# A tuned mixer and gated MLP block on one core: down products added to the output by adding DMAs, in 2x2 block form for all tokens, with the work of the MLP loop spread one slot apart

## The chip, the core and the metric

The kernel runs on one core of a Trainium2 chip. The metric is the device time of one execution in microseconds (us). Before the change the median of three runs is 1683.22 us (1682.0 to 1684.33). All matrix products are of 128 rows by 128 columns of weights against 512 tokens, in float32 rounded to a short form ("high") plus a remainder ("low").

## The reference, cut to what matters

```python
g = sigmoid((x * gate_w).sum(-1, keepdims=True))
a = linear_attention(x, wqkv, w_phi) @ wo          # 32 heads, per-head softmax feature maps
gate = x @ W_gate ; up = x @ W_up                  # x: 2048 x 576, W_gate, W_up: 576 x 4608
h = relu(gate) * up
out = g * a + (1 - g) * (h @ W_down)               # W_down: 4608 x 576
```

The kernel folds 1 - g into x ahead of the MLP (its square root into each factor), and keeps the output transposed: 576 rows, 2048 tokens.

## The kernel before

**Two stages.** The first makes the attention part and, in `project_out`, writes g * a transposed to a DRAM tile `att`. The second is the MLP, a loop `chunk(u)` over 72 units. A unit is one half of the tokens (`hf`, 1024 tokens, two blocks `t` of 512) and one of 36 chunks of 128 hidden columns; u = 0 to 35 work on the first half, 36 to 71 on the second. Two units make a group `g`, 36 groups in all.

**A unit's products.** Gate and up of a chunk for both token blocks are a 2x2 by 2x2 block product, done with seven products of sums and differences of blocks (in place of eight). `SEQ = (1, 5, 6, 2, 7, 3, 4)` is their order, one in each of a unit's seven slots, each of seven matmuls (`product`). The products accumulate in three PSUM tiles: `cx` (1, 6, 7, 4), `ca` (5, 3) and `cy` (2). ScalarE (ACT) copies `cx` or `ca` out while it still grows (tiles `g1`, `u2`, `g2`), VectorE (DVE) adds the rest, applies the gate, and `high_h`/`low_h` split a hidden tile into `hh` (ACT) and `hl` (DVE).

**Weights of the products.** For u below 36, the raw chunk `wr` is loaded, and unit u prepares the operands of unit u + 1: `blocks` (three blocks, high on ACT, low on DVE), `sums_of_blocks` (four DVE operations in place), `block_sums` (four sums, high and low). These operands, tiles `wb` and `ws`, are also written to DRAM (`wbd`, `wsd`), and the second half of the tokens loads them from there (`load_operands`).

**Down products.** Behind each slot's product stands a down product of the group before. For groups of the first half, `down_plain` multiplies plain blocks: eight slots of a group with six matmuls, and two with four for the last 64 output rows (`pm`): 56 matmuls. For groups of the second half, `down` uses the seven-product form for each half `m` of the output rows: 14 slots with three matmuls, four of them with two more for the last rows: 50 matmuls. Its weights need sums of blocks (`down_sums_of_blocks`, on GpSimd, POOL) and sums of hidden tiles. Both accumulate in two PSUM banks, `chain` and `other`, and DVE adds each bank into an accumulator `ac` in SBUF one slot later (L920 and L952). The accumulators are loaded from `att`, and stored to the output at the end of a token half.

**Order.** `in_order` keeps every engine's instructions in the order in which the Python code issues them, so an instruction that waits holds up all that stand behind it on its engine. Some of a unit's work is handed over to the next unit in lists (`CARRY`). In units 4 to 16 POOL also scales and subtracts x for the second half of the tokens (`second_half`, tiles `xb`, L296 and L301).

Of the kernel before, what the change touches and what calls it, by code (L numbers as in the profile page):

```python
# [7 lines left out]
F32 = mybir.dt.float32  # L8
# [54 lines left out]
def gated_mix_kernel(  # L63
# [33 lines left out]
    att = dram.tile([D, S], F32, name="att")  # L97
# [4 lines left out]
    wbd = dram.tile([NC, P, 3, 5, P], F32, name="wbd")  # L102
    wsd = dram.tile([NC, P, 4, 5, P], F32, name="wsd")
# [486 lines left out]
    def project_out(tb):  # L590
        oh, ol = OW.pop(tb)
        ts = slice(tb * TB, (tb + 1) * TB)
        for m in range(5):
# [17 lines left out]
            nc.sync.dma_start(att[m * P:m * P + n, ts], o)  # L611
# [96 lines left out]

    def load_operands(u):

        c = units[u][1]
        b, o = wop.tile([P, 3, 5, P], F32R, name="wb"), wop.tile([P, 4, 5, P], F32R, name="ws")
        nc.sync.dma_start(b.bitcast(F32), wbd[c])
        nc.sync.dma_start(o.bitcast(F32), wsd[c])
        WO[u] = {1: (b, 0), 2: (b, 1), 4: (b, 2), 5: (o, 2), 6: (o, 0), 7: (o, 3), 3: (o, 1)}
# [72 lines left out]
    tp = ctx.enter_context(tc.tile_pool(name="tp", bufs=7, **CB))  # L788
    ac = ctx.enter_context(tc.tile_pool(name="ac", bufs=1, **CB))
# [9 lines left out]
    LAST = {3: (0, 1), 2: (0, 0), 7: (1, 1), 4: (1, 0)}  # L799
    WDR, WD, W4, HID, ACC, ACC4, BANK, REST = {}, {}, {}, {}, {}, {}, {}, {}  # L800
# [3 lines left out]
    def load_down(g):  # L804
        if g < 2 * NG:
            WDR[g] = wdp.tile([P, 9 * P], F32, name="wdr", bufs=1)
            nc.sync.dma_start(WDR[g], wd[g % NG])
# [7 lines left out]
    def down_blocks(g, m, f):  # L815

        if f is high:
            o = down_tile()
# [37 lines left out]
    def plain_down(g, f):  # L856

        if f is high:
            o = down_tile()
            WD[g] = o[:, :16 * P].rearrange("p (s q) -> p s q", s=2)  # L860
            W4[g] = o[:, 16 * P:].rearrange("p (b s q) -> p b s q", b=2, s=2)
        f(WD[g], WDR[g][:, :8 * P])
        f(W4[g].rearrange("p b s q -> p s b q"), WDR[g][:, 8 * P:].rearrange("p (b q) -> p b q", b=2))

# [15 lines left out]
    def load_acc(hf, i, m, t):  # L880
        a = ACC[hf, i, m, t] = ac.tile([P, TB], F32, name=f"ac{i}{m}{t}")
        nc.sync.dma_start(a, att[rows(i, m, t, hf)])

    def load_rest(hf):
        for t in range(2):
            a = ACC4[hf, t] = ac.tile([64, TB], F32, name=f"ar{t}")
            nc.sync.dma_start(a, att[4 * P:, rows(0, 0, t, hf)[1]])

    PLAIN = {1: (0, 0, 1), 2: (0, 1, 1), 3: (2, 0, 1), 4: (0, 0, 0), 5: (0, 1, 0), 6: (2, 0, 0),
             8: (1, 0, 1), 9: (1, 1, 1), 11: (1, 0, 0), 12: (1, 1, 0)}  # L890

    def down_plain(g, s):

        if s not in PLAIN:
            return lambda: []
        i, m, t = PLAIN[s]
        first, last = g == 0, g == NG - 1
        mms = []
        if i == 2:
            if first:  # L900
                REST[t] = pm.tile([P, TB], F32, name=f"pm{t}")
            ps = REST[t]
            for c in range(2):
                w = W4[g][:, c].rearrange("p s q -> p (s q)")
                mms += [(w, v) for v in HID[g, c, t]]
        else:
            ps = pd.tile([P, TB], F32, name="chain" if s % 2 else "other")
            for c in range(2):
                b = 4 * m + (c if i == 0 else 3 - c)
                w = slice(b * P, (b + 1) * P)  # L910
                h, l = HID[g, c, t]
                mms += [(WD[g][:, 0, w], h), (WD[g][:, 0, w], l), (WD[g][:, 1, w], h)]
        for k, (w, v) in enumerate(mms):
            nc.tensor.matmul(ps, w, v, start=k == 0 and (i < 2 or first),  # L914
                             stop=k == len(mms) - 1 and (i < 2 or last), skip_group_check=True)

        def add():
            if i < 2:
                a = ACC[0, i, m, t]
                tt(out=a, in0=ps, in1=a, op=ADD)  # L920
                if last:
                    return [(0, i, m, t)]
            return []
        return add

    def down(g, s, bank):
# [22 lines left out]
        def add():  # L949
            i, t = ADDS[n]  # L950
            a = ACC[hf, i, m, t]
            tt(out=a, in0=ps, in1=a, op=ADD)  # L952
            return [(hf, i, m, t)] if last and LAST.get(n) == (i, t) else []
        return add

    def store(keys):
        for hf, i, m, t in keys:
            nc.sync.dma_start(out[rows(i, m, t, hf)], ACC.pop((hf, i, m, t)))
            if hf == 0:
                load_acc(1, i, m, t)  # L960

    def rest_rows(hf, t):

        b = tp.tile([64, TB], F32, name="b", tag="tp")
        nc.scalar.activation(b, REST[t][64:], AF.Copy)
        tt(out=b, in0=REST[t][:64], in1=b, op=ADD)
        for a in (ACC4[hf, 0], ACC4[hf, 1])[t:t + 1 if hf == 0 else 2]:
            pt(out=a, in0=a, in1=b, op=ADD)

    def store_rest(hf, t):  # L970
        nc.sync.dma_start(out[4 * P:, rows(0, 0, t, hf)[1]], ACC4[hf, t])

    def one_bank(m, n):
        key = "chain" if n == 1 else "other"
# [41 lines left out]
    CARRY = {j: [] for j in range(7)}  # L1016
    PEND = []

    def chunk(u):
        hf, c = units[u]  # L1020
        g, odd = divmod(u, 2)
        v = u + 1
        make = 0 < u < NC - 1
        plain = hf == 0
        done = []

        def slot(j, ps, n, first):

            product(ps, u, n, first)
            if PEND:  # L1030
                done.extend(PEND.pop()())
            if g > 0:
                q = g - 1
                PEND.append(down_plain(q, 7 * odd + j) if q < NG else down(q, 7 * odd + j, one_bank))
            store(done)
            done.clear()
            if u == 1 and j == 0:
                CARRY[3] += CARRY[0]
                CARRY[0].clear()
            work = CARRY[j][:]  # L1040
            CARRY[j].clear()
            for f in work:
                f()


        cx = px.tile([P, TB], F32, name="cx")
        slot(0, cx, 1, True)
        if u == 1:
            nc.sync.dma_start(wbd[u], WB.pop(u).bitcast(F32))
        if make:  # L1050
            blocks(v, high_w)
        elif NC - 1 <= u < 2 * NC - 1:
            load_operands(v)
        g1 = tp.tile([P, TB], F32, name="g1", tag="tp")
        nc.scalar.activation(g1, cx, AF.Copy)
        if make:
            blocks(v, low_w)
            blocks(v, low_w_rows)
        swap_in(u, 0)
        if u == 0:  # L1060
            next(early, None)

        ca = pa.tile([P, TB], F32, name="ca")
        slot(1, ca, 5, True)
        if u == 1:
            nc.sync.dma_start(wsd[u], WS.pop(u).bitcast(F32))
        if make:
            sums_of_blocks(v)
        u2 = tp.tile([P, TB], F32, name="u2", tag="tp")
        nc.scalar.activation(u2, ca, AF.Copy)  # L1070
        swap_in(u, 1)
        if u == 0:
            next(early, None)

        slot(2, cx, 6, False)
        if make:
            nc.sync.dma_start(wbd[v], WB.pop(v).bitcast(F32))
            block_sums(v, high_w)
        g2 = tp.tile([P, TB], F32, name="g2", tag="tp")
        nc.scalar.activation(g2, cx, AF.Copy)  # L1080
        if odd and plain and g > 0:
            plain_down(g, high)
        elif odd and g > 0:
            down_blocks(g, 0, high)
            down_blocks(g, 0, low)
            rest_weights(g, 0)
            rest_weights(g, 1)
        if units[u] == (1, 1):
            rest_rows(0, 0)
        swap_in(u, 2)  # L1090
        if u == 0:
            next(early, None)

        cy = py.tile([P, TB], F32, name="cy")
        slot(3, cy, 2, True)
        if odd and plain and g > 0:
            plain_down(g, low)
        elif odd and g > 0:
            down_sums_of_blocks(g, 0)
        tt(out=g1, in0=cy, in1=g1, op=ADD)  # L1100
        swap_in(u, 3)
# [233 lines left out]
```

## Time and profile before

| | |
|---|---|
| median of the runs | 1683.22 us |
| the profiled execution, and its span | 1685.55 us, 1683.8 us |
| mean granted TensorE clock in it | 0.983 |
| first matmul of the MLP loop | 417.06 us |
| last matmul | 1678.34 us |
| DVE, ACT, POOL busy over the span | 1256.9, 592.3, 213.8 us |

The loop has some three quarters of the span. A view by windows gives, for a stretch of time, each engine's busy time and the number of its instructions that began there. Matmuls are pipelined: a row of one matmul says 0.39 us, but the next begins 0.227 us after it, so the number of matmuls in a window tells more than the busy time.

### The profile page before, as it was taken

What the parts mean: (1) busy time and instruction counts of PE and PEld (TensorE: products, weight loads), DVE (VectorE), ACT (ScalarE), POOL (GpSimd) and SP (SyncE); (2) the same over time, 40 slices, a digit from 0 to 9 for tenths busy, and PEclk for the clock granted to TensorE, in tenths of its full rate; (3) what the DMA queues carried; (4) which work ended last, traced back from release to release, by engine and by line L of the source; (5) the groups of instructions that cost most, each with busy time, mean ns of one, the idle gap of its engine ahead of it and who ended that gap; (6) DMA issues with size and microseconds to landing.
All of it is one profiled execution on the core that took longest, in us unless ns stands there. A gap on an engine that the chain in (4) does not pass through costs nothing.

```text
span 1683.8 us, 20063 instructions
## 1 busy us (share of the span) xinstructions
PE 1624.7 (96%) x7726; PEld 1357.8 (81%) x7726; DVE 1256.9 (75%) x1881; ACT 592.3 (35%) x962; POOL 213.8 (13%) x257
## 2 busy tenths in 40 slices
PE   8999998798999999999999999999999999999997
PEld 8898996666787878777888887788888888888886
DVE  4878766565777887887877777677777777777777
ACT  4234336554333333233332333332333233323322
POOL 0118210002002010111000000311111111111111
PEclk9899998799999999999999999999999999999999
DMA  7214213544965556656655557654444434343432
GB/s 259 63 44 159 68 38 102 166 148 144 359 223 198 205 194 217 245 192 211 220 187 205 183 199 273 217 210 157 159 151 151 163 153 154 148 167 148 160 142 71
DMA packets 64476, 288.42 MB, mean 171 GB/s; under 512 B 6826, under 2 KB 16426, under 8 KB 55164
## 3 DMA queue, kind: packets, MB, share of 16 engines
q1 hardware_dynamic: 64380, 287.14, 47.6%
q8 instruction: 60, 0.98, 0.2%
q14 instruction: 36, 0.29, 0.1%
HBM read 174.30 MB, written 110.85 MB: 169 GB/s over the span
## 4 chain that ended last, share of the span: by engine, by line
PE 65%; DVE 6%; DMA 2%; ACT 2%; issue 1%; SPq 0%; ACTq 0%; DVEq 0%
PE cx L874 24%; PE ca L874 12%; PE cy L874 6%; PE chain L937 5%; PE other L914 5%; PE chain L914 5%; PE other L937 4%; PE pm L937 2%; PE pm L914 1%; DVE wb L680 1%; DVE wb L683 1%; DMA xt<-xb 1%; ACT wb L677 1%; DVE ac L952 1%; DVE wr L698 0%
## 5 line engine op out<-in xcount | busy, mean ns | idle before, releaser
L981 ACT ACTIVATE hh<-g 128x512 fp32r<-128x512 f32 x198 | 122.8, 629 | 538.0 <-DVE g L1124 296.0
L874 PE MATMUL cx<-xo,ws 128*128 128x512 f32 x1008 | 253.2, 390 | 11.7 <-ACT g L1080 11.7
L874 PE MATMUL ca<-xo,ws 128*128 128x512 f32 x1008 | 254.8, 392 | 0.2 <-DMA ws<-wsd 0.2
L874 PE MATMUL cx<-xo,wb 128*128 128x512 f32 x1008 | 249.3, 390 | 2.8 <-DVE o L610 1.8
L874 PEld LDWEIGHTS cx<-xo,ws 128*128 128x128 f32 x1008 | 188.6, 188 | 54.5 <-ACT g L1080 15.1
L874 PEld LDWEIGHTS ca<-xo,ws 128*128 128x128 f32 x1008 | 191.1, 190 | 40.9 <-DMA ws<-wsd 0.6
L874 PEld LDWEIGHTS cx<-xo,wb 128*128 128x128 f32 x1008 | 189.0, 188 | 42.9 <-DVE o L610 2.3
L986 DVE TENSOR_TENSOR hl<-g,hh 128x512 fp32r<-128x512 f32 x198 | 135.4, 691 | 37.2 <-ACT hh L981 32.1
L874 PE MATMUL cy<-xo,wb 128*128 128x512 f32 x504 | 125.9, 389 | 0.0
L937 PE MATMUL chain<-hh,wd 128*128 128x512 f32 x280 | 109.4, 391 | 3.4 <-DVE ac L952 1.9
L874 PEld LDWEIGHTS cy<-xo,wb 128*128 128x128 f32 x504 | 94.6, 188 | 19.7
L840 DVE TENSOR_TENSOR wd<-wdr,wd 128x384 fp32r<-128x384 f32 (+1 forms) x108 | 71.9, 680 | 50.0 <-ACT wd L837 50.0
L952 DVE TENSOR_TENSOR ac<-chain,ac 128x512 f32<-128x512 f32 x140 | 96.3, 688 | 17.0 <-PE chain L937 17.0
L914 PE MATMUL chain<-hh,wd 128*128 128x512 f32 x288 | 100.8, 391 | 3.4 <-DVE ac L920 3.4
L914 PE MATMUL other<-hh,wd 128*128 128x512 f32 x288 | 100.4, 389 | 0.0
L837 ACT ACTIVATE wd<-wdr 128x384 fp32r<-128x384 f32 (+1 forms) x108 | 63.7, 607 | 84.3 <-POOL wdr L829 81.3
L677 ACT ACTIVATE ws<-wr 128x1536 fp32r<-128x1536 f32 x36 | 53.6, 1488 | 100.0 <-DVE wr L701 89.5
L952 DVE TENSOR_TENSOR ac<-other,ac 128x512 f32<-128x512 f32 x105 | 72.0, 685 | 16.1 <-PE other L937 16.0
L937 PE MATMUL other<-hh,wd 128*128 128x512 f32 x210 | 81.7, 389 | 0.0
L1114 DVE TENSOR_TENSOR u<-cx,u 128x512 f32<-128x512 f32 x72 | 49.8, 691 | 32.0 <-PE cx L874 31.0
L1100 DVE TENSOR_TENSOR g<-cy,g 128x512 f32<-128x512 f32 x72 | 49.4, 686 | 27.2 <-PE cy L874 26.3
L1123 DVE TENSOR_TENSOR g<-ca,g 128x512 f32<-128x512 f32 x72 | 49.7, 691 | 26.0 <-PE ca L874 25.1
(239 smaller groups left out, 3172.8 us busy)
## 6 DMA issues: line engine op xcount, KB each, us to landing
wsd<-ws SPq DMA_DIRECT2D x36, 1280.0 KB
ws<-wsd SPq DMA_DIRECT2D x36, 1280.0 KB
wbd<-wb SPq DMA_DIRECT2D x36, 960.0 KB
wb<-wbd SPq DMA_DIRECT2D x36, 960.0 KB
wr<-wgu SPq DMA_DIRECT2D x36, 768.0 KB
wdr<-wd SPq DMA_DIRECT2D x36, 576.0 KB
eT<-et SPq DMA_DIRECT2D x12, 594.0 KB
er<-eT SPq DMA_DIRECT2D x12, 594.0 KB
```

The costliest lines, as they stand in the source:

```text
L677: nc.scalar.activation(o[:, :, 0:3], a, AF.Copy)
L837: nc.scalar.activation(o[:, 0], a, AF.Copy)
L840: tt(out=o[:, 1], in0=a, in1=o[:, 0].bitcast(F32), op=SUB)
L874: nc.tensor.matmul(ps, w, v, start=first and m == 0, stop=m == len(pairs) - 1, skip_group_check=True)
L914: nc.tensor.matmul(ps, w, v, start=k == 0 and (i < 2 or first), stop=k == len(mms) - 1 and (i < 2 or last), skip_group_check=True)
L937: mm = lambda ps, w, v, a, z: nc.tensor.matmul(ps, w, v, start=a, stop=z, skip_group_check=True)
L952: tt(out=a, in0=ps, in1=a, op=ADD)
L981: nc.scalar.activation(h, src, AF.Copy)
L986: tt(out=l, in0=src, in1=h.bitcast(F32), op=SUB)
L1100: tt(out=g1, in0=cy, in1=g1, op=ADD)
L1114: tt(out=u2, in0=cx, in1=u2, op=ADD)
L1123: tt(out=g2, in0=ca, in1=g2, op=ADD)
```

## The change

- **The output is the accumulator.** `project_out` writes to `out`. Each down slot's PSUM bank is copied by ACT into one of five SBUF tiles `sp`, and a DMA issued from POOL adds that tile to 128 rows by 512 tokens of `out` in DRAM (`accum_op=ADD`). There are 498 such DMAs. The tiles `att`, `ac` and `ar` are gone with their loads and stores, and so are DVE's additions of the banks.
- **One form of down for all tokens.** `plain_down` and `down_plain` are gone; all 36 groups use `down`, 50 matmuls.
- **Weights are made twice.** `wbd` and `wsd` are gone; units of the second half load `wr` and prepare operands as those of the first half do.
- **A new order.** `chunk` becomes `step(u, j)`, written slot by slot: what a slot of PE feeds is used by ACT and DVE in the next slot, copies of PSUM ahead of weight work, and of two dependent operations the second mostly stands one slot behind the first. The last group gets a written-out order, in which the output rows of `m` = 1 are loaded, added to in SBUF, and stored. Tiles `wdr` get two buffers, `tp` nine in place of seven.

```diff
+    def add_to_output(a, where):
+        nc.gpsimd.dma_start(out[where], a, accum_op=ADD)
...
         def add():
             i, t = ADDS[n]
-            a = ACC[hf, i, m, t]
-            tt(out=a, in0=ps, in1=a, op=ADD)
-            return [(hf, i, m, t)] if last and LAST.get(n) == (i, t) else []
+            a = sp.tile([P, TB], F32, name="sp")
+            nc.scalar.activation(a, ps, AF.Copy)
+            add_to_output(a, rows(i, m, t, hf))
         return add
...
     def load_w(u):
-        if units[u][0] == 0:
+        if u < len(units):
...
+    def step(u, j):
...
+        ps, first = bank(SEQ[j])
+        product(ps, u, SEQ[j], first)
+        evict()
+        make = 0 < u < len(units) - 1
+        d1 = not odd and g > 0
...
+        elif j == 2:
+            T["u2"] = copy(ca, "u2")
+            if d1:
+                low_h((q, 3), ODD[q][2])
+                high_h((q, 7), ODD[q][0])
+                high_h((q, 2), ODD[q][3])
+            if make:
+                sums_of_blocks(v)
+        elif j == 3:
+            T["g2"] = copy(cx, "g2")
+            if make:
+                block_sums(v, high_w)
+            if d1:
+                minus(ODD[q][3], ODD[q][1])
+                low_h((q, 7), ODD[q][0])
+                down_blocks(q, 1, low)
+                down_sums_of_blocks(q, 1)
...
+        if g > 0:
+            PEND.append(down(q, 7 * odd + j, one_bank))
...
+        for n in (1, 5, 3, 4):
+            i, t = ADDS[n]
+            a = SUM[1, i, t] = room[1].pop()
+            nc.sync.dma_start(a, out[rows(i, 1, t, 1)])
...
+            if n in (3, 7, 2, 4):
+                if m == 0:
+                    add_to_output(a, rows(i, m, t, 1))
+                else:
+                    nc.sync.dma_start(out[rows(i, m, t, 1)], a)
```

`evict()` runs the `add` of the slot before; `copy`, `gated` and `minus` are ACT's copy of a PSUM tile, the gate, and a difference of two hidden tiles.

How the order moves, at three places. First PE, in the middle of the first half of the tokens: `cx`, `ca`, `cy` are products of a unit, `chain`, `other` and `pd` the banks of the down products. Before:

```order
L874 MATMUL cx<-xo,ws 128x512 x7
L914 MATMUL chain<-hh,wd 128x512
L914 MATMUL chain<-hl,wd 128x512
L914 MATMUL chain<-hh,wd 128x512 x2
L914 MATMUL chain<-hl,wd 128x512
L914 MATMUL chain<-hh,wd 128x512
L874 MATMUL ca<-xo,ws 128x512 x7
```

and now:

```order
L856 MATMUL cx<-xo,ws 128x512 x7
L876 MATMUL pd_5139<-hh,wd 128x512
L876 MATMUL pd_5139<-hl,wd 128x512
L876 MATMUL pd_5139<-hh,wd 128x512
L856 MATMUL ca<-xo,ws 128x512 x7
```

Six matmuls between two products became three; over 18 groups that is 18 x (56 - 50) = 108 matmuls fewer, and no other matmul comes or goes.

Second ACT, about one unit of the first half (`wb`, `ws` weights of the next unit, `g`, `u` copies of `cx` and `ca`, `wd` down weights, `hh` hidden tiles). Before:

```order
L677 ACTIVATE wb<-wr 128x3x384
L1055 ACTIVATE g_7265<-cx 128x512
L1070 ACTIVATE u_7288<-ca 128x512
L677 ACTIVATE ws<-wr 128x4x384
L1080 ACTIVATE g_7308<-cx 128x512
L837 ACTIVATE wd<-wdr 128x1024
L837 ACTIVATE wd<-wdr 128x2x64
L981 ACTIVATE hh<-g_7308 128x512
L981 ACTIVATE hh<-g_7265 128x512
```

and now:

```order
L674 ACTIVATE wb<-wr 128x3x384
L891 ACTIVATE sp<-pd_5918 128x512
L965 ACTIVATE g_5935<-cx 128x512
L914 ACTIVATE hh<-g_5830 128x512
L828 ACTIVATE wd<-wdr 128x384
L891 ACTIVATE sp<-pd_5945 128x512
L965 ACTIVATE u_5961<-ca 128x512
L914 ACTIVATE hh<-g_5675 128x512
L914 ACTIVATE hh<-g_5782 128x512
L891 ACTIVATE sp<-pd_5918 128x512
L965 ACTIVATE g_5988<-cx 128x512
L674 ACTIVATE ws<-wr 128x4x384
```

The copy of `cx` that stood behind the high part of `ws` (L1080) now stands ahead of it, and a copy of a down bank to `sp` has been added in every slot.

Third POOL, in the second half of the tokens, with the semaphores that an instruction waits on; `wdr` are raw down weights, `ar` an accumulator of the last 64 output rows. Before:

```order
L968 TENSOR_TENSOR ar_4033<-ar_4033,b 64x512 [waits DVE_49]
L826 TENSOR_TENSOR wdr<-wdr 128x128 [waits DVE_49]
L827 TENSOR_TENSOR wdr<-wdr 128x128 [waits Pool_49]
L828 TENSOR_TENSOR wdr<-wdr 128x128 [waits Pool_49]
L829 TENSOR_TENSOR wdr<-wdr 128x128 [waits Pool_49]
```

and now:

```order
L817 TENSOR_TENSOR wdr<-wdr 128x128 [waits DVE_49]
L818 TENSOR_TENSOR wdr<-wdr 128x128 [waits Pool_49]
L819 TENSOR_TENSOR wdr<-wdr 128x128 [waits Pool_49]
L820 TENSOR_TENSOR wdr<-wdr 128x128 [waits Pool_49]
L863 DMA outT<-sp 128x512 [waits DMASW1_49,DMASW0_49,Activation_49]
L863 DMA outT<-sp 128x512 [waits DMASW7_49,DMASW2_49,Activation_49]
L863 DMA outT<-sp 128x512 [waits DMASW6_49,DMASW3_49,Activation_49]
L863 DMA outT<-sp 128x512 [waits DMASW4_49,Activation_49]
```

Between the sums of down weights POOL now issues one adding DMA per slot; each waits for ACT's copy, and many for the landing of earlier adding DMAs (DMASW), those to the same rows among them.

More of the change, by code (lines that the diff above doesn't have):

```diff
@@ L610, in project_out @@
                 tt(out=o, in0=b, in1=ps[:64], op=ADD)
-            nc.sync.dma_start(att[m * P:m * P + n, ts], o)
+            nc.sync.dma_start(out[m * P:m * P + n, ts], o)
             yield
@@ L707, in block_sums @@
         f(WS[u], RAW[u])
[L709 to L715, printed above, removed]
     order = [NTB - 1, *range(NTB - 1)]
@@ L878, in rows @@
         return slice(r, r + P), slice((2 * hf + t) * TB, (2 * hf + t + 1) * TB)
[L880 to L924, printed above, removed]
+    def add_to_output(a, where):
+        nc.gpsimd.dma_start(out[where], a, accum_op=ADD)
     def down(g, s, bank):
@@ new lines, in gated_mix_kernel, with evict, minus, gated @@
+    PEND, EVEN, ODD = [], {}, {}
+    STEPS = [(u, j) for u in range(len(units)) for j in range(7)]
+    def evict():
+        if PEND:
+            PEND.pop()()
+    def minus(a, b):
+        tt(out=b, in0=a, in1=b, op=SUB)
+    def gated(g, up):
+        nc.vector.scalar_tensor_tensor(out=g, in0=g, scalar=0.0, in1=up, op0=ALU.max, op1=MULT)
+    def copy(ps, name):
+        a = tp.tile([P, TB], F32, name=name, tag="tp")
+        nc.scalar.activation(a, ps, AF.Copy)
+        return a
+    BANKS = {}
@@ new lines, in bank, with prepare_down @@
+    def bank(n):
+        pool, name, new = {1: (px, "cx", 1), 6: (px, "cx", 0), 7: (px, "cx", 0), 4: (px, "cx", 0),
+                           5: (pa, "ca", 1), 3: (pa, "ca", 0), 2: (py, "cy", 1)}[n]
+        if new:
+            BANKS[name] = pool.tile([P, TB], F32, name=name)
+        return BANKS[name], bool(new)
+    def prepare_down(g, m, j):
+        if j == 0:
+            down_blocks(g, m, high)
+        elif j == 1:
+            down_blocks(g, m, low)
+        elif j == 2:
+            down_sums_of_blocks(g, m)
+        elif j == 4:
+            down_block_sums(g, m, high)
+        elif j == 5:
+            down_block_sums(g, m, low)
+        if m == 0 and j in (0, 1, 4, 5):
+            rest_weights(g, (0, 1, 4, 5).index(j))
@@ L1191, in gated_mix_kernel @@
         load_w(2)
-        for u in range(len(units)):
-            chunk(u)
+        for u, j in STEPS:
+            step(u, j)
         g = 2 * NG - 1
+        last_cx, o1 = LAST.pop()
+        o2 = LAST.pop()
+        e2, e1 = EVEN.pop(g)
+        room = [xr.tile([P, 3, TB], F32, name="xr", tag="xr") for _ in range(2)]
+        room = [[sp.tile([P, TB], F32, name="sp") for _ in range(4)],
+                [room[0][:, 0], room[0][:, 1], room[0][:, 2], room[1][:, 0]]]
+        SUM = {}
+        evict()
+        for n in (1, 5, 3, 4):
+            i, t = ADDS[n]
+            a = SUM[1, i, t] = room[1].pop()
+            nc.sync.dma_start(a, out[rows(i, 1, t, 1)])
         def banks(m, n):
```

359 lines of the change are left out of this document (139 added, 220 removed).

## The prediction

> **What bounds the kernel now.** I read the engines' totals, then windows, then PE's waits, then one stall instruction by instruction.
>
> ```profile
> PE 1624.7 (96%) x7726; PEld 1357.8 (81%) x7726; DVE 1256.9 (75%) x1881; ACT 592.3 (35%) x962; POOL 213.8 (13%) x257
> ```
> ```profile
> 500.00:550.00 50.00, 46.85 (x205) 37.98 (x204) 41.03 (x53) 16.58 (x23) 12.65 (x6) 1.00 0.58 206
> ...
> 850.00:900.00 50.00, 50.00 (x223) 41.39 (x222) 39.32 (x58) 15.96 (x22) 0.00 (x0) 1.00 0.54 195
> ...
> 1150.00:1600.00 450.00, 450.00 (x1985) 372.24 (x1984) 342.49 (x554) 137.39 (x272) 59.47 (x122) 1.00 0.41 154
> 1660.00:1670.00 10.00, 6.64 (x28) 4.64 (x27) 9.61 (x16) 3.35 (x6) 0.90 (x2) 1.00 0.00 0
> ```
>
> The columns are length, then busy time and count of PE, PEld, DVE, ACT, POOL, then granted clock, DMA share, GB/s. In the middle of either token half PE never rests at clock 1.00, with DVE at 39.32/50 = 79% and 342.49/450 = 76%, ACT near 31%. So matmuls set the time there, at 450/1985 = 0.227 us each. Two groups confirm it, the first half by ACT's `wb` (two units apart), the second by one product:
>
> ```profile
> 859.50 1.15 ACT L677 ACTIVATE wb<-wr 128x1152 fp32r<-128x1152 f32 x1
> ...
> 894.40 1.16 ACT L677 ACTIVATE wb<-wr 128x1152 fp32r<-128x1152 f32 x1
> ```
> ```profile
> 1225.67 1.59 PE cx L874 x7
> 1259.24 1.59 PE cx L874 x7
> ```
>
> A group takes 34.90 us in plain form (98 + 56 = 154 matmuls) and 33.57 us in block form (148). At 500 to 550 and at the end PE waits; the sums of its waits in the loop (us, times, longest):
>
> ```profile
> PE cx L874 <- ACT g L1080: 11.7, 8, 2.0
> PE chain L914 <- DVE ac L920: 3.4, 2, 1.9
> PE chain L937 <- DVE ac L952: 1.9, 2, 1.2
> ...
> PE chain L937 <- ACT hh L981: 1.5, 1, 1.5
> ```
>
> One of the eight:
>
> ```profile
> 502.74 8.10 POOL L296 TENSOR_TENSOR xb<-xb,sbp 128x768 f32<-128x768 f32 x4 [91.86 <-ACT u L1070]
> ```
> ```profile
> 502.56 0.56 DVE L699 TENSOR_TENSOR wr<-wr 128x384 f32<-128x384 f32 x1
> 503.15 2.08 DVE L700 TENSOR_TENSOR wr<-wr 128x384 f32<-128x384 f32 x1
> 505.27 2.08 DVE L701 TENSOR_TENSOR wr<-wr 128x384 f32<-128x384 f32 x1
> ```
> ```profile
> 507.44 1.49 ACT L677 ACTIVATE ws<-wr 128x1536 fp32r<-128x1536 f32 x1 [4.80 <-DVE wr L701]
> ```
>
> While POOL runs four operations on SBUF, a DVE operation that costs 0.56 costs 2.08; ACT's `ws` waits 4.80 for it, and the copy L1080, on which the next product waits, stands behind `ws`.
>
> **The change part by part.** *Fewer matmuls.* 18 groups lose 6 matmuls each: 108 x 0.227 = 24.5 us. The two group periods say 18 x (34.90 - 33.57) = 23.9. I take -24.3. It stands if ACT, DVE, POOL and DMA all fit into 33.57 us per group, for all 36 groups; so each is added up next.
>
> ```profile
> L986 DVE TENSOR_TENSOR hl<-g,hh 128x512 fp32r<-128x512 f32 x46 | 31.8, 692 | 18.0 <-ACT hh L981 16.1
> ...
> L680 DVE TENSOR_TENSOR ws<-wr,ws 128x1024 fp32r<-128x1024 f32 x23 | 28.0, 1216 | 0.0
> L680 DVE TENSOR_TENSOR wb<-wr,wb 128x768 fp32r<-128x768 f32 x22 | 22.4, 1019 | 8.1 <-ACT wb L677 8.1
> ...
> L683 DVE TENSOR_TENSOR ws<-wr,ws 32x512 fp32r<-32x512 f32 x23 | 15.7, 683 | 0.3
> ...
> L698 DVE TENSOR_TENSOR wr<-wr 128x384 f32<-128x384 f32 x22 | 13.8, 629 | 0.8
> ```
> ```profile
> L840 DVE TENSOR_TENSOR wd<-wdr,wd 128x512 fp32r<-128x512 f32 x18 | 12.3, 683 | 0.0
> ...
> L840 DVE TENSOR_TENSOR wd<-wdr,wd 128x384 fp32r<-128x384 f32 x18 | 10.0, 555 | 18.0 <-ACT wd L837 18.0
> ```
>
> *DVE per group:* 7 `low_h`, 4 differences, 6 additions from PSUM, 4 gates, 21 full-width at 0.69 = 14.5; weights of two units 2 x (1.02 + 1.22 + 2 x 0.68 + 4 x 0.63) = 12.2; down weights 2 x (0.68 + 0.56) = 2.5 and two small ones under 0.56, 0.5 together. Sum 29.7 of 33.57 us, 88%. The bank additions leave (14 x 0.69 a group in block form); in the second half the weights come instead. Every engine's order is fixed, so 88% hides only if no wait piles up. Its bounds are 0 (as at 79%) and 0.3 us per group, 11 us in all; I take +3, nearer to the full windows.
>
> What speaks against filling DVE is the 2.08 above. If POOL's eight sums of a group (4.4 us, below) held DVE for all their time, DVE would need 34.1 us, and the sum be 15 to 18 us worse. But in the second half these sums already run beside DVE, and there its rows are no longer than in the first (mean 692 ns in its row above, here 688):
>
> ```profile
> L986 DVE TENSOR_TENSOR hl<-g,hh 128x512 fp32r<-128x512 f32 x62 | 41.9, 688 | 2.5 <-ACT hh L981 1.4
> ```
>
> The Trainium skill (SBUF — State Buffer, "Who interferes with whom") has it as a rule: a DVE instruction with two SBUF inputs and a GpSimd instruction that reads SBUF exclude each other for a whole instruction. By that rule the 2.08 agrees, and the sum would be the worse one; the row of the second half does not bear out so much, so I keep +3 and make the rule's case a rival.
>
> ```profile
> L981 ACT ACTIVATE hh<-g 128x512 fp32r<-128x512 f32 x63 | 38.7, 628 | 121.1 <-DVE g L1150 71.4 <-DVE g L1124 25.9 <-DVE g L1166 23.5
> ...
> L837 ACT ACTIVATE wd<-wdr 128x512 fp32r<-128x512 f32 x18 | 11.4, 632 | 37.8 <-POOL wdr L829 37.8
> L1070 ACT ACTIVATE u<-ca 128x512 f32<-128x512 f32 x18 | 10.8, 598 | 9.3 <-PE ca L874 9.1
> ...
> L837 ACT ACTIVATE wd<-wdr 128x384 fp32r<-128x384 f32 x18 | 9.3, 514 | 0.0
> ```
>
> *ACT per group:* 7 `hh` at 0.63, 6 copies and 14 new copies to `sp` at 0.60, weights 2 x (1.15 + 1.49), down weights 2 x (0.63 + 0.51), three small ones under 0.51: 4.4 + 12.0 + 5.3 + 2.3 + 1.5 = 25.5 us, 76%. Hidden under PE, since a bank is written again two slots (4.8 us) after it was filled. Behind a copy that waits for a free `sp` stand `g1`, `u2` and `g2`, on which PE waits.
>
> ```profile
> L827 POOL TENSOR_TENSOR wdr<-wdr 128x128 f32<-128x128 f32 x17 | 11.4, 670 | 1.3
> ...
> L826 POOL TENSOR_TENSOR wdr<-wdr 128x128 f32<-128x128 f32 x17 | 7.9, 464 | 92.6 <-DVE wd L840 92.6
> ```
> ```profile
> 1071.08 3.50 DMA outT<-ac
> ```
> ```profile
> L958 SPq DMA_DIRECT2D outT<-ac x16: 332/383/825, 1060.6 to 1679.9; - x16
> ```
>
> *POOL per group:* eight sums, 2 x (0.67 + 3 x 0.46), and a small one: 4.4 us; new are 14 adding DMAs. The trace has none, nor any DMA issued by POOL. Call the issue X and the time to landing L. X has as its low end SP's issue of a 256 KB store, 0.38 us (the last row, median), as its high end POOL's longest operation above, 8.10/4 = 2.03. L has as low end that store's 3.50 us in the chain, as high end twice that, 7.0, if the sum is read back and then written. Of a half's seven down sums, the third and fourth go to the same rows one slot apart, so POOL sits out L twice a group: 14X + 2L + 4.4 must stay under 33.57. At L = 3.5 that holds up to X = 1.58, at L = 7 up to 1.08. Issuing is nearer to SP's row than to an operation over 768 columns: I take X = 1, L = 3.5 to 5, and cost 0. The five `sp` give 5 x 2.40 = 12 us from copy to reuse, enough for that. For the fixed part and the rate of a POOL-issued DMA the Trainium skill (DMA: Bandwidth & Descriptors, "Anatomy of one DMA — SWDGE (gpsimd) path") gives 2.0 us plus bytes/436 GB/s, so by it 2.6 us for 256 KB, an estimate without the addition, which no run here shows; the sum would stay the same.
>
> ```profile
> q1 hardware_dynamic: 64380, 287.14, 47.6%
> ...
> wsd<-ws SPq DMA_DIRECT2D x36, 1280.0 KB
> ...
> wbd<-wb SPq DMA_DIRECT2D x36, 960.0 KB
> ...
> wr<-wgu SPq DMA_DIRECT2D x36, 768.0 KB
> ```
>
> *DMA.* 0.476 x 1683.8 us for 287 MB is 2.79 us of all 16 engines per MB. The weights' way to DRAM and back goes: 72 x 2240 KB, 165 MB; 36 loads of `wr` come, 28 MB. A group then moves two `wr` and a `wdr`, 2.2 MB or 6 us, and 3.7 MB of sums: 10 us at a store's price, 20 at twice it, full at 2.7 times it. Hidden. SP loses its waits for stores and issues loads early, and the loads and stores of `ac` (16 each) go; PE's waits above name none of them: 0.
>
> *Slots apart.* The copy L1080 now stands ahead of `ws`, and POOL's `xb` operations come one at a time between adding DMAs, each costing DVE some 1.5 us (2.08 - 0.56) instead of a burst. Of the 11.7 us I take -9; bounds 0 and -11.7. The 3.4 us (`chain` behind DVE) lie where the operands of x are swapped, which stays as full: 0, at best -3.4. *End.* DVE works 9.61 of 10 us at 1660 and PE loses 1.9 + 1.5 us; the order there is more even, but adds loads of output rows that must follow their last adding DMA: -2, bounds +2 and -3.4.
>
> Sum: -24.3 + 3 + 0 - 9 - 2 = -32.3, from the profiled 1685.55 to 1653.3; its run is 2.3 us above the median, so 1651.
>
> **The rivals.** *POOL's adding DMAs set the pace (slower).* For it: 498 of an unknown price in one queue, with two waits for landing a group; at X = 1.5 and L = 7 a group takes 21 + 14 + 4.4 = 39.4 us, +5.8 x 35 = +204: 1855. At L = 5.25, 35.9 us and 1733. Against it: 13% POOL now, and 2.7-fold room in the DMA engines. It decides from 34.4 us per group on, where 35 x 0.9 eats the gain. *DVE sets the pace.* For it: the rows with 2.08. If POOL's sums hold DVE up in full, a group takes 34.1 us, 0.5 x 36 = +18: 1669. If issuing adding DMAs held DVE too, at SP's 0.38 each, 5.3 us more: 39.4 us, slower. Against it: the second half's row. *The stalls stay.* If the waits of 11.7 only move: 1660.
>
> **How the numbers follow.** The forecast has 0.58, its own range 1639 (all stalls gone, -44) to 1668 (DVE +11, half the stalls). Stalls stay: 0.10. DVE: 0.08, 0.02 of it slower. POOL's DMAs: 0.24, of it 0.01 still faster, 0.02 within 0.2% (3.4 us, about what a measurement here can tell from no change), 0.21 slower. Faster 0.75, same 0.02, slower 0.23. The range goes from 1637 to 1720, up to the mild POOL case; some 0.15 lies above.
>
> **What would show it.** Right: in both halves groups of 33.6 us, ACT near 76%, DVE near 88%, POOL below 90% of a window, no waits of PE for ACT's copies at the `xb` operations. Wrong: ACT's copies to `sp` idle until a DMA; a POOL row of some 2 us per adding DMA; groups longer than 34.4 us; DVE rows of 2 us beside POOL; at the end a PE or DVE wait for `xr<-outT`.

## The result, and the profile after

The changed kernel takes 1831.62 us (median of 4 runs, 1825.57 to 1843.72), the kernel before 1683.78 us beside it: a ratio of 1.0881, 95% interval 1.0814 to 1.0947. It is 8.8% slower, 181 us over the forecast and above its range.

The engines' totals and the two big DMA queues of the profiled execution after (span 1842.0 us), from its page:

```profile
PE 1676.7 (91%) x7618; PEld 1362.3 (74%) x7618; DVE 1350.3 (73%) x1983; ACT 977.6 (53%) x1672; POOL 787.1 (43%) x912
...
q0 software_dynamic: 71456, 130.06, 50.3%
q1 hardware_dynamic: 44732, 142.95, 24.1%
...
L863 POOL DMA_DIRECT2D outT<-sp x498 | 438.9, 985 | 691.3 <-issue 263.7
L891 ACT ACTIVATE sp<-pd 128x512 f32<-128x512 f32 x490 | 288.0, 595 | 430.9 <-DMA outT<-sp 252.6
```

The 108 matmuls are gone (7726 to 7618). No engine is full: POOL has 43%. But the adding DMAs on POOL (L863) and ACT's copies to `sp` (L891) wait for hundreds of microseconds. By windows, with the columns as in the prediction:

```profile
850.00:900.00 50.00, 47.13 (x195) 37.46 (x196) 38.00 (x58) 28.49 (x50) 23.95 (x31) 0.97 0.88 165
1150.00:1600.00 450.00, 413.61 (x1680) 327.33 (x1679) 318.95 (x489) 249.32 (x430) 211.94 (x262) 0.94 0.84 146
```

Where PE did 1985 matmuls in 450 us it now does 1680: 148 x 450/1680 = 39.6 us a group, not 33.57. At the full windows' 0.2265 us, 1680 matmuls are 380.5 us. PE waits 450 - 413.6 = 36 us here, and for the other 33 us matmuls begin further apart; the clock, granted at half for 51 us in all by its records in the trace (0.94 in the mean), is some 26 of these.

What is waited for in the loop, by the waits of PE, ACT and POOL (us, times, longest):

```profile
PE cx L856 <- ACT g L965: 83.0, 63, 3.2
PE pd L876 <- ACT sp L891: 23.5, 30, 1.7
...
ACT sp L891 <- DMA outT<-sp: 252.6, 135, 4.9
ACT wd L828 <- POOL wdr L820: 149.7, 60, 4.3
...
POOL outT L863 <- issue: 263.7, 92, 7.6
POOL outT L863 <- DMA outT<-sp: 225.1, 43, 7.4
```

Read from below, this is the whole chain: POOL cannot issue; so no `sp` comes free and POOL's sums `wdr`, queued behind, are late; ACT stands at its copy or at `wd`; the copies `g` behind that are late, and PE waits. Of the 691 us that POOL idles before its adding DMAs, 225 end with a landing (the data of an earlier DMA has arrived). Another 264, "issue", are idle time for which the profile shows no releaser at all; the rest is mostly for ACT. One place of the second kind, by POOL's timeline and by the tile `sp` in two narrow windows:

```profile
956.48 2.68 POOL L863 DMA_DIRECT2D outT<-sp  x3 [1.00 <-ACT wd L828]
965.29 0.88 POOL L863 DMA_DIRECT2D outT<-sp  x1 [6.14 <-issue]
```
```profile
L863 POOL DMA_DIRECT2D outT<-sp x1: 887/887/887, 956.5 to 956.5; - x1
...
DMA to landing us min/median/max: 8.5/8.5/8.5
...
L863 POOL DMA_DIRECT2D outT<-sp x2: 1147/1280/1414, 957.1 to 957.7; - x2
...
DMA to landing us min/median/max: 9.0/9.3/9.6
```

Three adding DMAs go out back to back at 956.5, 957.1 and 957.7. Then POOL is idle until 965.3: the first landed at 956.5 + 8.5 = 965.0. Nothing more starts before. By the trace, 90 of the 92 waits of this kind end 0.31 us after an adding DMA has landed, with two others still in flight. For every issue between 1200 and 1360 us, the trace gives how many adding DMAs were in flight, the new one included (number of issues at each count):

```
                        1    2    3    4    5
changed kernel          9   12   38    -    -
```

Never four, with five `sp` tiles; in the whole kernel four occur at 2 of 498 issues, both beside one of the four smaller sums of 64 rows. The landing takes 6.1 us after the issue in the median (3.2 to 12.9).

### The profile page after: what moved, and what is told of

Its sections match the earlier page's. It is cut to its first block, busy times and chain, and to the rows that moved or that the text cites. A ratio compares the mean times of both kernels' runs of the same rounds, so it can differ in the third digit from the quotient of the medians.

```text
span 1842.0 us, 21721 instructions
## 1 busy us (share of the span) xinstructions
PE 1676.7 (91%) x7618; PEld 1362.3 (74%) x7618; DVE 1350.3 (73%) x1983; ACT 977.6 (53%) x1672; POOL 787.1 (43%) x912
## 3 DMA queue, kind: packets, MB, share of 16 engines
q0 software_dynamic: 71456, 130.06, 50.3%
## 4 chain that ended last, share of the span: by engine, by line
DMA 33%; PE 22%; POOL 17%; issue 15%; ACT 8%; DVE 4%; SPq 1%; POOLq 0%; ACTq 0%; DVEq 0%
DMA outT<-sp 31%; POOL outT L863 9%; PE cx L856 4%; PE pq L151 3%; PE pk L151 2%; PE pd L876 2%; ACT sp L891 2%; PE pv L151 2%; POOL wdr L818 2%; PE ca L856 2%; PE kv L361 2%; ACT ws L674 1%; POOL wdr L819 1%; PE pwo L151 1%; POOL wdr L817 1%
## 5 line engine op out<-in xcount | busy, mean ns | idle before, releaser
L863 POOL DMA_DIRECT2D outT<-sp x498 | 438.9, 985 | 691.3 <-issue 263.7
L891 ACT ACTIVATE sp<-pd 128x512 f32<-128x512 f32 x490 | 288.0, 595 | 430.9 <-DMA outT<-sp 252.6
L876 PE MATMUL pd<-hh,wd 128*128 128x512 f32 x994 | 401.6, 404 | 26.6 <-ACT sp L891 23.5
L876 PEld LDWEIGHTS pd<-hh,wd 128*128 128x128 f32 x994 | 193.1, 194 | 85.5 <-ACT sp L891 40.3
L919 DVE TENSOR_TENSOR hl<-g,hh 128x512 fp32r<-128x512 f32 x252 | 181.5, 720 | 95.2 <-ACT hh L914 95.0
L876 PE MATMUL pd<-hl,wd 128*128 128x512 f32 x497 | 198.8, 400 | 0.2 <-DVE hl L919 0.2
L677 DVE TENSOR_TENSOR ws<-wr,ws 128x1024 fp32r<-128x1024 f32 x72 | 102.2, 1419 | 58.7 <-ACT ws L674 58.7
L677 DVE TENSOR_TENSOR wb<-wr,wb 128x768 fp32r<-128x768 f32 x72 | 79.3, 1102 | 50.6 <-ACT wb L674 50.5
L876 PEld LDWEIGHTS pd<-hl,wd 128*128 128x128 f32 x497 | 96.6, 194 | 19.2 <-DVE hl L919 0.5
L674 ACT ACTIVATE ws<-wr 128x1536 fp32r<-128x1536 f32 x72 | 107.4, 1491 | 4.3 <-POOL wr L698 2.4
L831 DVE TENSOR_TENSOR wd<-wdr,wd 128x384 fp32r<-128x384 f32 (+1 forms) x142 | 92.4, 651 | 21.7 <-ACT wd L828 18.6
```

Source lines behind the costliest of these rows:

```text
L674: nc.scalar.activation(o[:, :, 0:3], a, AF.Copy)
L677: tt(out=o[:, :, 3:5], in0=a[:, :, 0:2], in1=o[:, :, 0:2].bitcast(F32), op=SUB)
L831: tt(out=o[:, 1], in0=a, in1=o[:, 0].bitcast(F32), op=SUB)
L863: nc.gpsimd.dma_start(out[where], a, accum_op=ADD)
L876: mm = lambda ps, w, v, a, z: nc.tensor.matmul(ps, w, v, start=a, stop=z, skip_group_check=True)
L891: nc.scalar.activation(a, ps, AF.Copy)
```

## The experiments

Four theories: **A**, the addition is slow in the DMA engines; **B**, two down sums of each half `m` go to the same rows one slot apart, and POOL sits out a landing; **C**, POOL lacks room for the descriptors of its DMAs (the list of transfers that an issue writes for the DMA engines), which the program sets to 1024 (bytes per partition) and the change left alone; **D**, there are too few `sp` tiles. Times are medians; each ratio is to the kernel before on the same chip.

**Stores in place of adding DMAs.** The output then holds only the last sum of each block.

```diff
-        nc.gpsimd.dma_start(out[where], a, accum_op=ADD)
+        nc.gpsimd.dma_start(out[where], a)
```

> The same 498 DMAs from POOL, but as plain stores: the addition in DRAM is left out, so the output holds only the last partial sum. Theory A (the addition in the DMA engines is slow: 1.86 us of each engine per 256 KB, against 0.73 for a store): landing falls from 6.1 us to about 3.5, the DMA share from 0.87 to below 0.6, the time to 1655 to 1680. Theory B (two sums for the same rows one slot apart make POOL sit out a landing): the same fall, since 14 x 0.9 + 2 x 3.5 + 7 = 27 us is under 33.6. Theory C (POOL's issuing, or the room for its descriptors, is what waits: 264 us of POOL's idle time has no releaser): stays at 1800 or more.

1651.64 us, ratio 0.9796 (0.9735 to 0.9857). Page, windows and tile `sp`:

```profile
q0 software_dynamic: 39712, 130.06, 20.8%
```
```profile
500.00:550.00 50.00, 50.00 (x222) 41.44 (x221) 45.91 (x66) 33.51 (x60) 23.03 (x36) 1.00 0.52 186
...
1150.00:1600.00 450.00, 450.00 (x1987) 372.59 (x1987) 374.97 (x578) 294.41 (x510) 172.26 (x311) 1.00 0.50 174
```
```profile
L863 POOL DMA_DIRECT2D outT<-sp x498: 538/542/735, 443.8 to 1645.9; - x166
...
DMA to landing us min/median/max: 2.2/3.0/8.0
```

With the addition gone and all else kept, including the waits for the same rows, the loop is full and the time is the forecast's. So all of the loss hangs on the addition. An adding DMA takes 71456/498 = 143.5 packets, a store 39712/498 = 79.7; of each of the 16 DMA engines 0.503 x 1842.0/498 = 1.86 us, a store 0.208 x 1651.6/498 = 0.69 us.

**Adding DMAs to other rows,** 16 output blocks in turn, so that no two close to each other meet; the sums land in wrong places.

```diff
-            add_to_output(a, rows(i, m, t, hf))
+            k, b = divmod(g % NG * 14 + s, 4)
+            k %= 4
+            add_to_output(a, (slice(k * P, (k + 1) * P), slice(b * TB, (b + 1) * TB)))
```

> Adding DMAs as before, but each goes to another of 16 blocks of the output in turn, so that none needs the landing of a recent one; the sums land in wrong places. Theory B: POOL's waits for landings go, 1655 to 1700. Theory A: the engines are as busy as before, and the five tiles sp wait for landings instead: 1780 or more. Theory C: no change, 1800 or more.

1709.15 us, ratio 1.0137 (1.0061 to 1.0214). The waits:

```profile
POOL outT L863 <- issue: 321.1, 133, 6.0
...
ACT sp L891 <- DMA outT<-sp: 141.9, 94, 4.9
```

POOL's waits for the landing of an adding DMA are gone, and 122 us of the loss with them. But the idle time without a releaser has grown, to 321 us, and the kernel is still slower than before: B is a part and not the whole.

**More room for POOL's descriptors,** and nothing else.

```diff
-    nc = bacc.Bacc(..., dynamic_dma_scratch_size=1024)
+    nc = bacc.Bacc(..., dynamic_dma_scratch_size=4096)
```

> Only the room for POOL's DMA descriptors is four times as large (4096 in place of 1024 bytes per partition). Theory C: the idle time without a releaser (264 us) goes, 1700 or less. Theories A and B: within 10 us of 1830.

1673.43 us, ratio 0.9933 (0.9905 to 0.996). The waits:

```profile
POOL outT L863 <- ACT sp L891: 323.1, 186, 17.4
POOL outT L863 <- DMA outT<-sp: 135.6, 34, 10.3
...
ACT sp L891 <- DMA outT<-sp: 52.4, 36, 3.7
```

One number takes 158 us off, and POOL's idle time without a releaser falls to 4.4 us. The DMA engines are as slow with an addition as before (landing 7.0 us in the median, queue q0 at 51.9%), so A alone is not it either.

**A sixth `sp` tile,** room 1024.

```diff
-    sp = ctx.enter_context(tc.tile_pool(name="sp", bufs=5, **CB))
+    sp = ctx.enter_context(tc.tile_pool(name="sp", bufs=6, **CB))
```

> Only six tiles sp in place of five. Theory D (too few tiles: ACT's copies wait 253 us for landings): a slot more of cover, 2.4 us for each of some 70 waits, so 100 us or more less, 1730 or less. Theory A: DMA engines stay at 0.87 busy, 10 to 40 us less. Theory B: POOL still sits out the same landings, 10 to 40 us less.

1787.3 us, ratio 1.0601 (1.0505 to 1.0696). D gives 44 of the 180 us: the copies on ACT stand less, but POOL still sits idle without a releaser for 220.1 us.

**Room 2048.**

> Room for descriptors 2048 bytes per partition. POOL's rows with 1024 show three adding DMAs back to back and then an idle time; if 1024 bytes hold three to four DMAs in flight, 2048 hold six to eight, and at a landing of 6 to 7 us and a DMA every 2.4 us three are in flight on average: 1670 to 1690, all but the gain of 4096. If room counts in another way (per byte, or by a share of the four-fold), halfway: about 1750.

1673.41 us, ratio 0.9922 (0.9895 to 0.9949): the same as with 4096.

**Room 4096 and other rows,** the second and third edits together.

> With 4096 bytes of room, the adding DMAs also go to other rows in turn (sums land in wrong places). If what is left over the plain stores (1673 against 1652) is POOL sitting out landings for the same rows (136 us of POOL's idle time): 1650 to 1660. If it is the DMA engines, 0.9 busy, and slower sums on POOL: 1665 to 1675.

1654.54 us, ratio 0.981 (0.9785 to 0.9835), 3 us above plain stores. PE is full from 1150 to 1600, with the DMA engines at 0.98:

```profile
1150.00:1600.00 450.00, 450.00 (x1987) 372.60 (x1986) 371.17 (x579) 294.01 (x510) 235.66 (x311) 1.00 0.98 175
```

So the two together account for the loss. They are not independent: more room takes off 158 us and other rows then 19, or other rows 122 us and more room then 55. The 3 us that stay over plain stores lie within the spread of these runs (1652.46 and 1656.61 against 1649.91 and 1653.36), so no further price of the addition in the DMA engines is seen here.

**Two sums in one tile.** The two down sums that meet the same rows one slot apart (the sixth and third of the seven products) are added by DVE in one `sp` tile and leave by one DMA: 12 a group in place of 14. Room 4096.

```diff
+            if n == 3:
+                a = HELD.pop()
+                tt(out=a, in0=ps, in1=a, op=ADD)
+            else:
...
+            if n == 6:
+                HELD.append(a)
+            else:
                 add_to_output(a, rows(i, m, t, hf))
```

> With 4096 bytes of room, the third and fourth down sum of a half, which go to the same rows, are added up in one sp tile (DVE adds the second from PSUM) and leave in one DMA: 12 instead of 14 adding DMAs a group, and no add to rows that were added to one slot earlier. DVE gets 1.4 us a group more (31.1 of 33.6). If waits for the same rows are the rest: 1655 to 1662. If DVE at 93% sets the pace: 1675 or more.

1661.42 us, ratio 0.9851 (0.9837 to 0.9866): faster than both kernels. What PE still loses in the loop is mostly at the swap of the operands of x between the token halves (1000 to 1100), as with plain stores:

```profile
1150.00:1600.00 450.00, 450.00 (x1987) 372.63 (x1986) 381.76 (x604) 281.88 (x485) 208.30 (x283) 1.00 0.88 160
1000.00:1100.00 100.00, 88.65 (x364) 71.03 (x363) 86.28 (x125) 62.19 (x103) 49.83 (x60) 0.93 0.83 180
```

**The kernel before with one copy moved:** the copy L1080 (there L1079) stands ahead of the high part of `ws`, as it does after the change; nothing else.

```diff
-            block_sums(v, high_w)
         g2 = tp.tile([P, TB], F32, name="g2", tag="tp")
         nc.scalar.activation(g2, cx, AF.Copy)
+        if make:
+            block_sums(v, high_w)
```

> The kernel before with one thing of the new order: ACT's copy of cx (L1080) ahead of the high part of ws. The forecast's term says -9 of the 11.7 us of PE's waits for that copy: 1673 to 1676. If DVE, held up by POOL, only makes another copy or sum late: no change, 1680 to 1685.

1679.69 us, ratio 0.9964 (0.9946 to 0.9982). Waits of PE:

```profile
PE cx L874 <- DVE u L1115: 7.4, 5, 2.7
...
PE cx L874 <- ACT g L1079: 1.9, 1, 1.9
```

The wait for the copy falls from 11.7 to 1.9 us, about as the forecast had it, but DVE, still held beside POOL's `xb`, is late next (0.9 us before, 7.4 now). The move alone is worth some 6 us. Which of the other moves takes DVE's share of the stall away was not tried apart.

**Two sums in one tile with room 1024.**

> Two of a half's seven down sums (the sixth and third, which go to the same rows one slot apart) are added in one sp tile, so 12 adding DMAs a group instead of 14 and no two next to each other on the same rows; the room for POOL's DMA descriptors stays at 1024 as in the changed kernel. Room theory (three adding DMAs in flight, each 6 us to land, so one per some 2.4 us with the queue's own gaps): 12 instead of 14 per group still wait for room; POOL keeps idle time that nothing releases (over 100 us) and the time stays at or above 1680 us. Rival, same rows one slot apart and the number of DMAs alone are what costs: about 1661 us, as with room 4096, and POOL without such idle time.

1659.38 us, ratio 0.9839 (0.9816 to 0.9862): as fast as with room 4096, so this expectation was wrong. The waits of POOL:

```profile
POOL outT L863 <- ACT sp L897: 364.1, 224, 19.1
...
POOL outT L863 <- DMA outT<-sp: 46.9, 28, 3.0
POOL outT L863 <- issue: 42.8, 39, 2.4
```

Its own figure, one adding DMA in some 2.4 us, gives 12 x 2.4 = 28.8 us a group, under the 33.57 that PE needs; I had not multiplied it out. With other rows and room 1024 the group is 33.57 + (1709 - 1652)/36 = 35.2 us, 2.5 us for each of 14. So a limit of three in flight acts as a rate: by this estimate 14 a group don't fit under PE and 12 do (30 us). With two waits a group for the same rows on top, as in the changed kernel, a group came to 39.6.

**A candidate:** two sums in one tile, room 2048, six `sp`; the sums of low parts of x at the swap on DVE in place of POOL; the last group's sums all leave by adding DMAs, without loads of output rows.

```diff
-            low_rest(1, i - 5, pt)
+            low_rest(1, i - 5, tt)
...
-            nc.sync.dma_start(a, out[rows(i, 1, t, 1)])
...
-                if m == 0:
-                    add_to_output(a, rows(i, m, t, 1))
-                else:
-                    nc.sync.dma_start(out[rows(i, m, t, 1)], a)
+                add_to_output(a, rows(i, m, t, 1))
```

> The paired sums with room 2048 and six sp tiles, and two more edits: the sums of low parts of x at the swap of its operands are done by DVE instead of POOL, and the last group's sums all leave by adding DMAs, with no output rows loaded first. If the waits of PE at the swap (11 us lost between 1000 and 1100) come from POOL's sums standing behind adding DMAs, 4 to 8 us less than the 1661.4 of the paired kernel: 1653 to 1657. If they come from DVE, already full there, or from the matmuls' own order: 1661 or slower, and PE's waits there name DVE. The end: 0 to -2 if the loads of output rows waited for their last adding DMA, +3 to +5 if the landing of an adding DMA (6 us) now ends the run instead of a store's.

1654.03 us, ratio 0.9807 (0.9793 to 0.9821), the fastest with nothing left out: 1.9% under the kernel before. The swap, by windows:

```profile
1000.00:1100.00 100.00, 91.84 (x387) 73.69 (x386) 90.57 (x138) 66.07 (x110) 43.37 (x57) 0.97 0.90 191
```

At the swap 23 more matmuls fit into the window than with the sums on POOL, 23 x 0.2265 = 5 us of the 7 between the medians. The end gave nothing in the profiled executions: from the last unit's `cy` product to the end of the span they take 34.7 us here and 32.8 with two sums in one tile at room 4096.

**Plain stores with room 512** (the addition left out, as in the first experiment).

> Plain stores from POOL (the addition is left out, so the output is not the reference's) as in e1, but with room 512 for POOL's DMA descriptors instead of 1024. If room for descriptors limits how many DMAs are in flight whatever they do: POOL shows idle time that nothing releases, as in the changed kernel (264 us there, none with plain stores and 1024), and the time rises over 1660 us. If the idle time belongs to the addition alone: 1652 us as in e1.

1651.27 us, ratio 0.9791 (0.9773 to 0.9809): no loss, as the second expectation had it. But this time does not clear the room for stores: with a landing of 3.0 us and one every 2.4 us some 1.3 in flight suffice. The trace shows the limit all the same. With room 1024 four or five stores are in flight at 37 of the 498 issues, with 512 never more than three, and once POOL stands without a releaser with three in flight:

```profile
644.22 0.54 POOL L863 DMA_DIRECT2D outT<-sp  x1 [4.77 <-ACT wd L828]
645.05 0.54 POOL L863 DMA_DIRECT2D outT<-sp  x1 [0.29 <-issue]
646.22 0.55 POOL L863 DMA_DIRECT2D outT<-sp  x1 [0.63 <-ACT u L965]
649.84 0.54 POOL L863 DMA_DIRECT2D outT<-sp  x1 [3.07 <-issue]
```

The first of these lands after 5.3 us, at 649.5, and the fourth starts 0.3 us later. So the limit does not belong to the addition; the addition makes it bind, since its DMAs take more packets and are in flight twice as long.

**Room 1536,** otherwise the changed kernel.

> The changed kernel with room 1536 for POOL's DMA descriptors in place of 1024, nothing else. In the trace of the changed kernel never more than three adding DMAs are between issue and landing, and a fourth starts 0.3 to 0.4 us after the first of them has landed; with room 2048 and 4096 there are up to five, as many as there are sp tiles. If the room sets that number in proportion, 1536 gives four (three and a half to five), POOL's idle time that nothing releases shrinks from 264 us to under 80, and the time lies between the two: 1673 to 1720 us. If the room is not in proportion to the number, but 1024 only falls below some least size: 1673 us, as at 2048. If room is taken in powers of two and the rest is lost: still three, and 1831 us.

1675.46 us, ratio 0.9948 (0.9925 to 0.9972), as at 2048, with 4.7 us of POOL's idle time without a releaser. The count in flight, as above (issues between 1200 and 1360 us):

```
                                1    2    3    4    5
changed kernel, room 1024       9   12   38    -    -
other rows, room 1024           -   11   52    -    -
six sp, room 1024               9   11   39    -    -
two sums in one, room 1024      2   18   38    -    -
room 1536                      10   10   13   27    7
room 2048                      10   10   13   23   11
room 4096                      10   10   17   24    6
two sums in one, room 4096      3   16   28    9    -
stores, room 1024              24   26   11    4    1
stores, room 512               23   27   16    -    -
```

With room 1024 there are never more than three adding DMAs here, whatever the rows or the tiles; with 1536 and more up to five, as many as there are tiles. That the room for descriptors sets the number is shown. Its size per DMA is inferred: an adding DMA has 9 packets for each of 16 engines (143.5/16), three fit into 1024, four do not, five fit into 1536, so a packet takes over 1024/36 = 28.4 and at most 1536/45 = 34.1 bytes. Stores, with 5 packets for each engine (79.7/16) and three in 512, agree: at most 512/15 = 34.1. The Trainium skill (DMA: Bandwidth & Descriptors, "SWDGE vs HWDGE vs iDMA") says that a DMA issued from GpSimd has its descriptors, a pair for each operation, appended to rings in SBUF, and its "Terms" make one 16 bytes: 32 bytes a pair, which lies between these bounds. That the room counts both descriptors of a pair is not shown.

## Why the prediction was wrong, point by point

- **Fewer matmuls, -24.3: right.** 108 fewer, and with plain stores the loop runs full at 0.2265 us a matmul.
- **DVE, +3, and ACT, 0: they hide, where POOL lets them.** With plain stores DVE has 374.97/450 = 83% (88% forecast), ACT 294.41/450 = 65% (76%; its rows overlap, so that adding up their durations gave too much), and PE rests nowhere from 1150 to 1600.
- **Slots apart, -9, and the end, -2: near in sum, in part by luck.** All waits of PE from the loop on come to 21.7 us before and 15.5 us with plain stores: -6.2, against -8 for the three terms +3, -9 and -2 together. The wait for the copy went from 11.7 to 1.8 us, and from 450 to 1000 us PE does 2428 matmuls, 49 more than before. But at the swap, which the forecast had at 0, it does 50 fewer, 11 us. First before, then with plain stores:

```profile
1000.00:1100.00 100.00, 96.64 (x417) 78.92 (x416) 72.56 (x101) 37.50 (x59) 17.03 (x14) 0.98 0.65 232
```
```profile
1000.00:1100.00 100.00, 89.92 (x367) 72.31 (x366) 85.95 (x121) 64.60 (x109) 41.95 (x64) 0.93 0.57 199
```

  The longest wait there is for POOL's `xo`, 4.8 us.
- **DMA, "10 us at a store's price, 20 at twice, full at 2.7 times": the price is 1.86/0.69, 2.7 times** by the two pages of the profile. The engines are then 84% to 98% busy and PE can still be full (other rows, room 4096). Hidden, by a hair.
- **POOL, "X = 1, L = 3.5 to 5, and cost 0": the step that failed.** X was near: 0.88 us where no other holds it. L is 6.1 to 7.0 us, over what the forecast took and at the upper end of its bounds, and the sums `wdr` rose too (below). Yet 14 x 0.88 + 2 x 6.1, 8 sums for 6.6 us and the small one for 0.7 are 31.8 us: with the landing of this kernel the formula still says hidden. What it lacks is a limit on DMAs in flight. It took each DMA to cost POOL its issue, and the two a group for the same rows a landing. With three in flight and 6 us to land, POOL also sits out landings that it does not depend on; room alone takes back 158 of the 180 us.
- **"The five `sp` give 12 us from copy to reuse, enough for that": wrong in the first half of the tokens.** Where two sums meet the same rows, the second waits out the landing of the first and then lands itself: 2 x 7.0 = 14 us, over 12. Other rows take off 19 us at room 4096. The two profiled executions lie 14 us apart: 10 of these have come up when the second half of the tokens begins, none is added until its last unit, and 4 come in the written-out last group. With room 4096 and the rows kept:

```profile
450.00:1000.00 550.00, 542.03 (x2374) 443.93 (x2373) 489.89 (x690) 352.34 (x608) 316.23 (x386) 1.00 0.94 189
1150.00:1600.00 450.00, 450.00 (x1987) 372.73 (x1986) 370.73 (x577) 292.82 (x508) 235.56 (x310) 1.00 0.93 175
```

  In the first stretch ACT waits 47.5 us for a free `sp`, in the second not at all, though there too a group has its two waits for the same rows. In the first POOL also has the operations on `xb`, DVE is 489.89/550 = 89% busy and a landing takes 7.4 us, not 6.8; which of these makes the difference was not tried apart.
- **The rivals.** "POOL's adding DMAs set the pace" came true in direction (0.24); of its two groups of 35.9 and 39.4 us the measured 39.6 is nearest to the upper. That is luck: its way there, X = 1.5, is not what happened. The sign that the forecast named, ACT's copies idle until a DMA, is the largest wait of ACT.
- **"DVE rows of 2 us beside POOL": there, and on both sides.** POOL's sums of down weights in the loop:

```profile
L817 POOL TENSOR_TENSOR wdr<-wdr 128x128 f32<-128x128 f32 x72 | 70.9, 985 | 0.1
L818 POOL TENSOR_TENSOR wdr<-wdr 128x128 f32<-128x128 f32 x72 | 64.9, 902 | 5.6
```
```profile
951.36 1.84 POOL L817 TENSOR_TENSOR wdr<-wdr 128x128 f32<-128x128 f32 x1
```
```profile
951.12 1.78 DVE L677 TENSOR_TENSOR ws<-wr,ws 128x1024 fp32r<-128x1024 f32 x1
```

A sum of 0.46 us takes 1.84 beside a DVE operation with two SBUF inputs, which takes 1.78 for its 1.22. That the two hold each other up agrees with the rule of the Trainium skill that the prediction weighed (SBUF — State Buffer, "Who interferes with whom"); that one runs at its full speed while the other stands, as an exclusion for a whole instruction would have it, these rows do not show, since both are longer. It hurt POOL more than DVE, whose `hl` rows went from 692 to 720 ns; with plain stores PE was full beside it.

- **The Trainium skill's fit for a DMA from GpSimd** (DMA: Bandwidth & Descriptors, "Anatomy of one DMA — SWDGE (gpsimd) path"), 2.6 us for 256 KB, is near the plain store's 3.0 us; for an adding DMA it is less than half of the 6.1 measured.

## What to carry to other kernels

Count the DMAs of a queue that must be in flight at once (landing time over the time between two issues, plus what has piled up behind a wait for the same rows), and compare this with the room for their descriptors; here the addition made the landing twice as long and took nearly twice the packets. Idle time on POOL that nothing releases, after a few DMAs in a row, ending as an earlier one lands, was the sign of too little room here, and either more room (one number) or fewer sums cured it. Two sums to the same rows were better added on chip than sent one behind the other (1661 against 1673 us at room 4096).

## What the runs showed of the hardware that I had not expected

- An adding DMA of 256 KB from SBUF to DRAM, against a plain store issued from POOL: 0.87 against 0.54 us of issue, 143.5 against 79.7 packets, 6.1 to 7.0 against 3.0 us to land, 1.86 against 0.69 us of each DMA engine.
- Room 1024 holds three of them, and POOL then stands still with all behind it; 1831.62 us against 1675.46 at room 1536, with nothing more at 2048 or 4096.
- Short waits of PE can cost more than their length. In the changed kernel the waits between 1150 and 1600 us come with a granted clock of 0.94. By the clock's records in the trace it fell to half ten times there, for 51 us in all, in steps of 3.41 us, each time behind a step of 3.41 us in which PE had idled for 1.75 us or more. One such place, and with six `sp` the whole stretch:

```profile
1380.00:1390.00 10.00, 7.38 (x31) 5.28 (x29) 6.38 (x12) 4.48 (x9) 3.64 (x5) 1.00 0.78 99
1390.00:1400.00 10.00, 9.21 (x28) 7.38 (x29) 5.48 (x9) 4.95 (x8) 7.42 (x10) 0.66 0.71 93
```
```profile
1150.00:1600.00 450.00, 422.08 (x1802) 333.78 (x1801) 335.45 (x522) 263.65 (x464) 215.58 (x279) 1.00 0.90 159
```

  With six `sp` PE waits 28 us in the same stretch, at most 2.9 at once, and the clock stays at 1.00: one step of 3.41 us held 1.87 us of idle time there, no other over 1.65. In the changed kernel no step with up to 1.58 us was followed by a fall. So the sum of the waits does not decide, but how much falls into one step; where the limit lies is not shown more closely. The Trainium skill (TensorE: Matmul & The Clock Gate, "What's actually happening") lets the clock fall after an idle window of some 3.4 us; the waits in the changed kernel were each shorter (at most 3.2 us), and the clock was granted lower all the same.
